# A fused state-space and feed-forward kernel: six gate/up tiles of the first 256 tokens ahead of the rest, with two token tiles transposed by DMA

## The chip, the cores and the metric

The kernel runs on one core of one Trainium2 chip. The metric is the device time of one execution in microseconds (us). A core has five engines that each run their own instructions in order: TensorE (PE, with its weight loads PEld), VectorE (DVE), ScalarE (ACT), GpSimd (POOL) and SyncE (SP). DMAs are issued from an engine's queue (SPq, ACTq, POOLq) and moved by 16 DMA engines.

## What is computed

```python
x = A_x                                   # [1, 2048, 512] bf16
xn = layernorm(x)                         # over the last axis, eps 1e-5
# A: diagonal complex state space, 512 states
dt = exp(log_dt); Lam_bar = exp(dt * Lam); B_bar = ((Lam_bar - 1) / Lam)[:, None] * Bmat
Bu = einsum("bld,pd->blp", xn, B_bar)
h[t] = Lam_bar * h[t-1] + Bu[:, t]        # 2048 steps
y = 2 * einsum("blp,dp->bld", h, Cmat).real + xn * Dskip
# B: feed-forward, hidden width 1376
z = (silu(xn @ w_gate) * (xn @ w_up)) @ w_down
out = x + y + z
```

All inputs and the output are bf16.

## The kernel before

**Tiles.** The 2048 tokens are 16 token tiles of 128 and 4 chunks of 512. The hidden width of 1376 is 10 feature tiles of 128 and a last one of 96. A feature tile of a chunk takes 8 matmuls with 512 columns: 4 for gate and 4 for up, one for each 128 of the 512 inputs (`gateup_tile`, L491; `gu_mm`, L429). ScalarE then empties the two banks of PSUM, gate through silu into `guT` and up as a copy into `u2` (`gu_out`, L440), and VectorE multiplies the two for a pair of feature tiles at once (L451). B-projection (`bproj_tile`, L352) is 8 such groups of 4 matmuls a chunk, each emptied by ScalarE (L359). PSUM has a pool of 8 banks (L69), and every matmul group takes its bank from it (`bank()`, L73).

**The head, tokens 0 to 511** (L599 to L684). PE starts with 9 dummy matmuls of 512 columns, while the first token tile is loaded. The norm of token tiles 0 to 3 runs on VectorE and ScalarE (`ln_stats`, L184; `rstd_act`, L188: Ln with a bias tile `eps_t`, then Exp; `norm_dve`, L201). Each of the four tiles is transposed on PE (`xT_pe`, L213: four transposes of 128x128, two to a bank), and the banks are copied to `xnT` by VectorE or ScalarE (L227, L229). Three feature tiles (H = 3) are begun at once, in six held banks (`held`, L603): `head_mm` (L627) gives one of gate and up a range of token tiles, in an order written out by hand (L635 to L671), so that PE has work as each token tile arrives. The transpose of the parameter rows (`prm_transpose`, L249) stands in the same bank as one of these. When token tile 3 is in, the held tiles are finished and emptied one by one (L679 to L683). Feature tiles 3 to 6 of chunk 0 follow (L741), then B-projection of chunk 0 (L745), then tiles 7 to 10 (L760).

**The parameters.** `params_a`, `params_a2` and `params_sin` (L252 to L312) make the decay and the angles; on ScalarE they are two Exp, one load of an activation table (L259) and two Sin, all ahead of the first silu. `params_b` (L314) is 17 small operations on VectorE that make the factors of C; they are used by `c_ops` (L331), which make `CF` ahead of the first `out_ssm` (L538).

**The planner.** Work of VectorE and ScalarE that isn't tied to a matmul group (the norm of the other chunks, the sine tables, the rotations and scans, the C factors) lies in `backlog` as pairs of a cost and an operation. After each group of matmuls `pump(us)` (L580) adds the group's PE time to `owed` and takes operations from the front of the backlog while `owed` is at least half the cost of the next one. `multiply` (L588) does the products that are due and takes 0.65 off `owed` for each. `need(tag)` (L594) empties the backlog up to a tag. So the emitted order of VectorE and ScalarE follows from the costs and from the order of the groups on PE.

**The queues.** SP issues nearly all loads (L123 to L148): x of tiles 0 and 2, gate and up of the weight groups, x of tiles 4 to 7, eight transposing loads of the B matrices into `BT` (L142), the last weights (`w_last`, L147). ScalarE issues x of tiles 1 and 3 and the first up group (L125 to L129). The weights lie in groups of feature tiles (`fgroups`, L88: 2, 1, 4 and 3 tiles). Token tiles 4 and on are transposed by DMA from SP (`xT_dma`, L232), as their norm is done; `load_late` (L150) and the transposes of C (L766) follow on SP.

## Time and profile before

| what | value |
|---|---|
| time, median of 3 | 179.23 us (179.14 to 179.45) |
| span of the profiled execution | 177.3 us |
| PE busy | 172.9 us, 97% of the span |
| DVE, ACT, POOL busy | 154.4, 94.7, 23.2 us |
| first transpose on PE | 4.76 us |
| first matmul with 256 columns | 7.68 us |
| load of the second activation table | 10.00 us, 1.28 long |
| first silu | 11.51 us |
| first matmul of feature tile 3 | 11.73 us |
| first matmul of feature tile 6 | 16.91 us |
| first matmul of B-projection | 18.64 us |
| DMA transposes of token tiles 4 to 7 issued | 20.06 to 25.2 us |
| DMA | 15.53 MB in 29131 packets |

The profile is of one execution, and its span goes from the first to the last instruction of the program; the time of an execution is 1.9 us longer. Times in the views are counted from the start of the span. "L631" is line 631 of the kernel before. A row of a group gives busy time, the mean length of one instruction in ns, and the idle time of the engine ahead of it with the one that ended it. Matmuls overlap, so the mean length of one isn't what it costs in a row of many.

### The profile page before, as it was taken

How to read it: one execution, taken by the hardware profiler on the slowest of the kernel's cores; microseconds unless marked ns; L12 is line 12 of the kernel's file. 1: busy time of each engine (PE TensorE's matmuls, PEld its weight loads, DVE VectorE, ACT ScalarE, POOL GpSimd, SP SyncE). 2: the span in 40 equal slices, each digit the busy share in tenths (PEclk: the TensorE clock that was granted, in tenths of full speed). 3: DMA queues.
4: the chain of work that ended last, by engine and by line, in shares of the span. 5: the costliest groups of instructions: out<-in, count | busy, mean ns of one | idle time of the engine just before them, and what ended most of it. 6: DMA issues, size and time to landing. Idle time of an engine off the chain costs nothing.

```text
span 177.3 us, 2449 instructions
## 1 busy us (share of the span) xinstructions
PE 172.9 (97%) x900; PEld 83.6 (47%) x916; DVE 154.4 (87%) x238; ACT 94.7 (53%) x173; POOL 23.2 (13%) x29
## 2 busy tenths in 40 slices
PE   8999999999999999999999999999999999999993
PEld 2884444444444444444444444444444444444743
DVE  6789997999999977899999999999999999990033
ACT  4589696977499369914966662013766600220000
POOL 6003000001200140000700000014280000150000
DMA  5999749973041024900440000005469500072012
GB/s 163 316 264 239 148 90 261 334 126 89 0 96 26 0 52 96 355 0 0 60 62 2 0 0 4 0 0 61 58 97 177 86 0 0 0 85 33 4 50 69
DMA packets 29131, 15.53 MB, mean 88 GB/s; under 512 B 18848, under 2 KB 29056, under 8 KB 29088
## 3 DMA queue, kind: packets, MB, share of 16 engines
q1 hardware_dynamic: 24416, 11.41, 28.8%
q0 software_dynamic: 3456, 3.28, 13.7%
q10 hardware_dynamic: 1248, 0.69, 1.3%
q8 instruction: 7, 0.11, 0.3%
q14 instruction: 4, 0.03, 0.1%
HBM read 8.03 MB, written 5.24 MB: 75 GB/s over the span
## 4 chain that ended last, share of the span: by engine, by line
PE 98%; issue 1%; DVE 0%
PE ps L432 36%; PE ps L528 19%; PE ps L545 16%; PE ps L357 16%; PE ps L631 3%; PE ps L608 2%; PE ps L483 2%; PE ps L535 2%; PE ps L472 1%; PE ps L220 1%; DVE res L548 0%; PE ps L250 0%
## 5 line engine op out<-in xcount | busy, mean ns | idle before, releaser
L432 PE MATMUL ps<-xnT,wg 128*128 128x512 bf16 x144 | 37.8, 379 | 0.4
L432 PE MATMUL ps<-xnT,wu 128*128 128x512 bf16 x145 | 37.3, 379 | 0.0
L528 PE MATMUL ps<-wd_sb,guT 128*128 128x512 bf16 (+2 forms) x177 | 36.7, 355 | 0.2
L399 DVE TENSOR_TENSOR_SCAN g<-r_t,car,u 128x512 bf16<-128x512 f32 x24 | 28.8, 1264 | 0.0
L545 PE MATMUL ps<-CF,wt 128*128 128x512 bf16 (+2 forms) x141 | 28.2, 355 | 0.2
L357 PE MATMUL ps<-xnT,BT 128*128 128x512 bf16 x126 | 28.2, 379 | 0.1
L446 ACT ACTIVATE guT<-ps 128x512 bf16<-128x512 f32 x40 | 24.6, 615 | 5.0 <-PE ps L432 5.0
L447 ACT CAST u<-ps 128x512 bf16<-128x512 f32 x40 | 24.1, 602 | 5.2 <-PE ps L432 5.1
L528 PEld LDWEIGHTS <-guT 128*128 128x128 bf16 x180 | 16.9, 98 | 18.0
L432 PEld LDWEIGHTS <-wu 128*128 128x128 bf16 x148 | 14.5, 98 | 17.5
L432 PEld LDWEIGHTS <-wg 128*128 128x128 bf16 x148 | 14.4, 98 | 17.2
L555 ACT CAST res<-ps 128x512 bf16<-128x512 f32 x12 | 6.7, 594 | 28.1 <-PE ps L545 28.1
L556 POOL DMA_DIRECT2D out_dram<-res x12 | 10.5, 1041 | 78.0 <-ACT res L555 78.0
L545 PEld LDWEIGHTS <-wt 128*128 128x128 bf16 x144 | 13.4, 98 | 14.4 <-issue 0.4
L357 PEld LDWEIGHTS <-BT 128*128 128x128 bf16 x128 | 12.5, 98 | 15.1
L359 ACT CAST u<-ps 128x512 bf16<-128x512 f32 x32 | 17.6, 588 | 3.7 <-PE ps L357 3.6
L451 DVE TENSOR_TENSOR guT<-guT,u 128x1024 bf16<-128x1024 bf16 x20 | 13.5, 680 | 0.0
L548 DVE TENSOR_TENSOR res<-ps,xn_end 128x512 bf16<-128x512 f32 (+2 forms) x6 | 3.0, 514 | 11.8 <-PE ps L545 11.8
L195 POOL TENSOR_TENSOR rstd<-ve,neg_half 128x4 f32<-128x4 f32 x3 | 5.3, 1761 | 53.9 <-DVE ve L194 53.9
L367 DVE TENSOR_TENSOR pm<-u,c 128x2048 bf16<-128x2048 bf16 x8 | 9.8, 1221 | 1.2 <-ACT c L284 1.1
L185 DVE BATCH_NORM_STATS2 stats<-xall 128x6 f32<-128x512 bf16 x14 | 9.5, 676 | 0.4 <-DMA xall<-in_A_x_dram 0.4
L367 DVE TENSOR_TENSOR pm<-g,c 128x2048 bf16<-128x2048 bf16 x8 | 9.7, 1215 | 0.1
(108 smaller groups left out, 166.6 us busy)
## 6 DMA issues: line engine op xcount, KB each, us to landing
out_dram<-in_A_x_dram SPq DMA_DIRECT2D x1, 1536.0 KB, 7.0
out_dram<-res POOLq DMA_DIRECT2D x12, 128.0 KB, 3.0
out_dram<-xall POOLq DMA_DIRECT2D x3, 512.0 KB, 7.6
wd_sb<-in_B_w_down_dram SPq DMA_DIRECT2D x1, 1280.0 KB, 10.9
xall<-in_A_x_dram SPq DMA_DIRECT2D x1, 1024.0 KB, 6.1
xall<-in_A_x_dram SPq DMA_DIRECT2D x2, 256.0 KB, 4.6
wg<-in_B_w_gate_dram SPq DMA_DIRECT2D x1, 512.0 KB, 5.6
wu<-in_B_w_up_dram SPq DMA_DIRECT2D x1, 512.0 KB, 6.1
```

What stands on the lines that cost most here:

```text
L185: nc.vector.bn_stats(out=stats[:, n, :], in_=xall[:, n, :])
L357: nc.tensor.matmul(ps[:], lhsT=BT[:, part, k, q * 128:(q + 1) * 128], rhs=xnT[:, k, c * CW:(c + 1) * CW], start=(k == 0), stop=(k == KD - 1))
L359: nc.scalar.copy(out=u_tiles[c][:, part, q, :], in_=ps[:])
L367: V.tensor_tensor(out=t[:], in0=flat(src()[:, i]), in1=flat(tab[:]), op=ALU.mult)
L399: V.tensor_tensor_scan(out=g()[:, part, q, :], data0=r_t[:, q:q + 1].to_broadcast([128, CW]), data1=u_tiles[c][:, part, q, :], initial=ini ...
L432: nc.tensor.matmul(ps[:fs, lo:hi], lhsT=wslice(groups, fi, k), rhs=xnT[:, k, c * CW + lo:c * CW + hi], start=(k == 0), stop=(k == KD - 1))
L446: nc.scalar.activation(out=guT[:fs, fi, :], in_=psg[:fs], func=ACT.Silu)
L447: nc.scalar.copy(out=u_pair[c][:fs, fi % 2, :], in_=psu[:fs])
L451: products.append(lambda: V.tensor_tensor(out=g, in0=g, in1=u, op=ALU.mult))
L528: nc.tensor.matmul(o[:], lhsT=gu_tiles[c][:, fi, i * 128:(i + 1) * 128], rhs=wd_sb[:, fi, lo:hi], start=(fi == 0), stop=False)
L545: nc.tensor.matmul(o[:], lhsT=w_tiles[c][:, part, q, i * 128:(i + 1) * 128], rhs=CF[:, part, q, lo:hi], start=False, stop=(c > 0 and part ...
L556: nc.gpsimd.dma_start(out=out_v[:, n, :], in_=res[:], accum_op=ALU.add)
```

## The change

It re-orders the head. Six feature tiles instead of three are begun in the six held banks, as three pairs (0, 2), (1, 3), (4, 5): a bank now holds one of gate and up for two feature tiles and 256 tokens, where it held one feature tile and 512 tokens. First all six are computed for tokens 0 to 255; then `head_out` empties a pair's two banks for that half, and the pairs are computed for tokens 256 to 511 in banks taken again from the pool (`second`). Products are done by half, with 512 elements instead of 1024.

Token tiles 2 and 3 are transposed by DMA from SP, not on PE. The norm of tiles 0 and 1 is done in two halves of 256 columns, and both copies of tile 0 are VectorE's, both of tile 1 ScalarE's. The bias of the Ln is the number 1e-5 instead of a tile.

Loads: the weight groups have 2 feature tiles each; ScalarE issues groups 1, 2 and 3, with group 2 between the two `rstd_act` of tiles 0 and 1 and group 3 after that of tile 3. SP issues, behind the two transposes, x of tiles 4 to 7 in one DMA, the eight transposing loads of B, and group 4. `w_last` is issued by GpSimd, out of the backlog. `params_b` moves to GpSimd, except for its reciprocal. The backlog begins with one table operation ahead of the norm's statistics, and eight feature tiles instead of seven stand ahead of B-projection.

```diff
-    fgroups = [(0, 2), (2, 3), (3, 7), (7, FT - 1)]
+    fgroups = [(0, 2), (2, 4), (4, 6), (6, 8), (8, FT - 1)]
...
-    load_w1(nc.sync, wg_g, wg_v, 1)
-    load_w1(nc.sync, wu_g, wu_v, 1)
+    load_w1(nc.scalar, wg_g, wg_v, 1)
+    load_w1(nc.scalar, wu_g, wu_v, 1)
...
+    def load_mid():
+        nc.sync.dma_start(out=xall[:, TPC:2 * TPC, :], in_=x_v[:, TPC:2 * TPC, :])
+        for part, src in enumerate((A_B_re, A_B_im)):
+            for k in range(KD):
+                nc.sync.dma_start_transpose(out=BT[:, part, k, :], in_=src[:, k * 128:(k + 1) * 128])
+        load_w1(nc.sync, wg_g, wg_v, 4)
+        load_w1(nc.sync, wu_g, wu_v, 4)
+
+    def load_w_last():
+        nc.gpsimd.dma_start(out=w_last[:, :, 0:LB + LA], in_=wg_v[:, :, FL:F])
+        nc.gpsimd.dma_start(out=w_last[:, :, LB + LA:128], in_=wu_v[:, :, FL + LB:F])
...
-        nc.scalar.activation(out=ve[:, n:n + 1], in_=mv[:, n, 1:2], func=ACT.Ln, bias=eps_t[:, 0:1])
+        nc.scalar.activation(out=ve[:, n:n + 1], in_=mv[:, n, 1:2], func=ACT.Ln, bias=EPS)
...
     def params_b():
+        G = nc.gpsimd
...
-        tt(t_a[:], lre, lre, ALU.mult)
+        gt(t_a[:], lre, lre, ALU.mult)
...
         V.reciprocal(out=den[:], in_=den[:])
...
+    def head_mm(sets, fis, which, lo, hi, ks=range(KD)):
+
+        base = lo * 128 // HALF * HALF
         for fi in fis:
+            p, j = place[fi]
             for k in ks:
+                nc.tensor.matmul(sets[p][which][:, j, lo * 128 - base:hi * 128 - base],
+                                 lhsT=wslice((wg_g, wu_g)[which], fi, k),
                                  rhs=xnT[:, k, lo * 128:hi * 128], start=(k == 0), stop=(k == KD - 1))
...
+    def head_out(sets, p, half):
+
+        if half == 0:
+            head_u[p] = up_p.tile([128, 2, CW], BF16, name="u2")
+        cols = slice(half * HALF, (half + 1) * HALF)
+        a, b = pairs[p]
+        g, u = gu_tile(0)[:, a:b + 1:b - a, cols], head_u[p][:, :, cols]
+        nc.scalar.activation(out=g, in_=sets[p][0][:], func=ACT.Silu)
+        nc.scalar.copy(out=u, in_=sets[p][1][:])
+        products.append(lambda: V.tensor_tensor(out=g, in0=g, in1=u, op=ALU.mult))
...
     ln_stats(0)
     rstd_act(0)
+    load_w1(nc.scalar, wg_g, wg_v, 2)
     nc.vector.bn_stats(out=stats[:, 1, :], in_=xall[:, 1, :])
-    norm_dve(0)
+    norm_dve(0, 0, DH)
+    norm_dve(0, DH, D)
     nc.vector.bn_aggr(out=mv[:, 1, :], in_=stats[:, 1, :])
     rstd_act(1)
-    xT_pe(0, on_dve=(0,))
-    dummy(4, 128)
-    norm_dve(1)
+    load_w1(nc.scalar, wu_g, wu_v, 2)
+    xT_pe(0, 0, True)
+    dummy(1, 128)
+    xT_pe(0, 1, True)
+    dummy(3, 128)
+    norm_dve(1, 0, DH)
+    norm_dve(1, DH, D)
     ln_stats(2)
+    head_mm(held, (0, 1), 0, 0, 1, kh[0])
+    head_mm(held, (0, 1), 0, 0, 1, kh[1])
+    xT_pe(1, 0, False)
+    head_mm(held, (0, 1), 1, 0, 1, kh[0])
+    xT_pe(1, 1, False)
+    head_mm(held, (0, 1), 1, 0, 1, kh[1])
     rstd_act(2)
     nc.vector.bn_stats(out=stats[:, 3, :], in_=xall[:, 3, :])
     norm_dve(2)
+    xT_dma(2)
     nc.vector.bn_aggr(out=mv[:, 3, :], in_=stats[:, 3, :])
     rstd_act(3)
+    norm_dve(3)
+    xT_dma(3)
+    load_w1(nc.scalar, wg_g, wg_v, 3)
+    load_w1(nc.scalar, wu_g, wu_v, 3)
+    load_mid()
+    head_mm(held, (0, 1), 0, 1, 2, kh[0])
+    head_mm(held, (0, 1), 1, 1, 2, kh[0])
+    head_mm(held, (0, 1), 0, 1, 2, kh[1])
+    head_mm(held, (0, 1), 1, 1, 2, kh[1])
+    head_mm(held, (2, 3), 0, 0, 2)
+    pp = prm_transpose()
+    head_mm(held, (2, 3), 1, 0, 2)
     params_a(pp)
     params_a2()
     params_sin()
+    head_mm(held, (4, 5), 0, 0, 2)
+    head_mm(held, (4, 5), 1, 0, 2)
     tables = table_ops()
     stats1, norm1 = ln_rest(1, False)
-    queue("ln1", stats1)
-    queue("tables", tables[:2])
+    queue("tables", tables[:1])
+    queue("ln1", stats1 + [(0.0, load_w_last)])
+    queue("tables", tables[1:2])
     queue("ln1", norm1)
     queue("tables", tables[2:])
+    second = []
+
+    def more():
+        second.append((bank((128, 2, HALF)), bank((128, 2, HALF))))
+
+    more()
+    head_out(held, 0, 0)
+    head_mm(second, pairs[0], 0, 2, 3)
+    head_mm(second, pairs[0], 1, 2, 3)
+    pump(GU / 2)
+    more()
+    head_out(held, 1, 0)
+    head_mm(second, pairs[1], 0, 2, 3)
+    head_mm(second, pairs[1], 1, 2, 3)
+    pump(GU / 2)
+    multiply(1)
+    head_out(held, 2, 0)
+    for p in range(2):
+        head_mm(second, pairs[p], 0, 3, 4)
+        head_mm(second, pairs[p], 1, 3, 4)
+        head_out(second, p, 1)
+        pump(GU / 2)
+        multiply(1)
+    more()
+    head_mm(second, pairs[2], 0, 2, 4)
+    head_mm(second, pairs[2], 1, 2, 4)
+    head_out(second, 2, 1)
+    pump(GU)
+    multiply(1)
...
-    G0 = 7
-    for fi in range(H, G0):
+    G0 = 8
+    for fi in range(2 * NP, G0):
```

More of the change, by code (lines that the diff above doesn't have):

```diff
@@ L211, with xT_pe @@
     HK = KD // 2
-    def xT_pe(n, on_dve=(), prm_too=False):
+    def xT_pe(n, h, on_dve):
         c, i = divmod(n, TPC)
-        for h in range(2):
-            tp = bank((128, HK * 128 + 128), BF16)
-            for k in range(HK):
-                lo = (h * HK + k) * 128
-                nc.tensor.transpose(out=tp[:, k * 128:(k + 1) * 128], in_=xn_tile(c)[:, i, lo:lo + 128],
-                                    identity=ident[:])
-            if prm_too and h == 1:
-                prm_transpose(tp[:, HK * 128:])
-            dst = xnT[:, h * HK:(h + 1) * HK, n * 128:(n + 1) * 128]
-            src = tp[:, 0:HK * 128].rearrange("p (k t) -> p k t", k=HK)
-            if h in on_dve:
-                nc.vector.tensor_copy(out=dst, in_=src)
-            else:
-                nc.scalar.copy(out=dst, in_=src)
-        return tp[:, HK * 128:]
+        tp = bank((128, HK * 128), BF16)
+        for k in range(HK):
+            lo = (h * HK + k) * 128
+            nc.tensor.transpose(out=tp[:, k * 128:(k + 1) * 128], in_=xn_tile(c)[:, i, lo:lo + 128], identity=ident[:])
+        dst = xnT[:, h * HK:(h + 1) * HK, n * 128:(n + 1) * 128]
+        src = tp[:].rearrange("p (k t) -> p k t", k=HK)
+        if on_dve:
+            nc.vector.tensor_copy(out=dst, in_=src)
+        else:
+            nc.scalar.copy(out=dst, in_=src)
     def xT_dma(n):
@@ L247, with prm_transpose @@
     V = nc.vector
-    def prm_transpose(pp):
-        nc.tensor.transpose(out=pp, in_=prm_rows[:], identity=ident[:])
+    def prm_transpose():
+        pp = bank((128, 128), BF16)
+        nc.tensor.transpose(out=pp[:], in_=prm_rows[:], identity=ident[:])
+        return pp
     def params_a(pp):
@@ L601 @@
     BP = 4 * 0.2163
-    H = 3
-    held = [(bank(), bank()) for _ in range(H)]
-    warm = held[0][0]
+    NP = 3
+    HALF = CW // 2
+    held = [(bank((128, 2, HALF)), bank((128, 2, HALF))) for _ in range(NP)]
+    warm = held[0][0][:].rearrange("p a b -> p (a b)")
     def dummy(n, cols):
@@ L684 @@
-    pump(2.0)
+    second = []
[19 more added lines that the diff above has]
+        multiply(1)
```

80 lines of the change are left out of this document (25 added, 55 removed).

## The prediction

> **What bounds the kernel now.** I read the page's busy times first, then the chain that ended last, then the waits, then the timeline of the first 20 us with that of TensorE's neighbours.
>
> ```profile
> PE 172.9 (97%) x900; PEld 83.6 (47%) x916; DVE 154.4 (87%) x238; ACT 94.7 (53%) x173; POOL 23.2 (13%) x29
> ...
> PE 98%; issue 1%; DVE 0%
> ```
>
> TensorE is the chain: nothing that another engine does is on it. All waits of PE until 40 us come to one, the start (0.8 us), and the chain in order of time has PE from 0.78 to 174.54. So the change can win only what it takes out of PE's own stream, or out of the small gaps at the start, and it loses whatever new wait it puts there. From the chain in order of time and the groups by shape:
>
> ```profile
> 4.78 0.59 PE ps L220 x4
> ...
> 8.28 0.22 PE ps L220 x4
> ...
> 9.66 0.22 PE ps L220 x4
> 9.88 2.01 PE ps L631 x36
> ...
> 25.71 5.18 PE ps L432 x24
> ```
>
> Columns: start, length, what. The rows give the price of one instruction in the stream: 2.01/36 = 0.056 us for 128 columns, 0.22/4 = 0.055 for a transpose, 5.18/24 = 0.216 for 512 columns. The 256-wide ones start four in 0.437 us (7.68 to 8.11 in the timeline): 0.109 each. The "mean" of the group of transposes (0.241 us) isn't the price: they overlap.
>
> ```profile
> 7.68 0.60 PE L631 MATMUL ps<-xnT,wg 128*128 128x256 bf16 x4
> ...
> 9.35 0.21 ACT L254 ACTIVATE dt_t<-prm 128x4 f32<-128x4 f32 x1 [0.81 <-DVE prm L253]
> ...
> 10.00 1.28 ACT L259 ACT_TABLE_LOAD   x1
> ...
> 11.51 0.58 ACT L446 ACTIVATE guT<-ps 128x512 bf16<-128x512 f32 x1
> ...
> 11.73 1.03 PE L432 MATMUL ps<-xnT,wg 128*128 128x512 bf16 x3
> ...
> 20.06 5.16 SPq L234 DMA_TRANSPOSE xnT<-xall  x4
> ```
>
> Here the reader is to see ScalarE: its first silu comes at 11.51, straight behind the table load, and no bank of `held` comes free before that. The last line prices a DMA transpose: 1.29 us of SP each; from issue to landing it took 2.4 us (all four alike, on a quiet queue).
>
> **The change, part by part.** I sum up to one mark: the first matmul of tile 6, now at 16.91 us. The profiled span is 177.3 us; the three timed executions took 179.14 to 179.45 (median 179.23), so some 1.9 us lie around the span, and I add them unchanged.
>
> *The start to the first 256-wide matmul (now 7.68).* The bias of the Ln becomes a number: the Ln with `eps_t` took 0.298, the Exp with no tile of bias 0.203, so 0.09 sooner. The half norm: 0.41 us for 512 elements and 0.17 for the 4 elements of the small tensor_scalars give 0.29 for 256, so 0.12 sooner. Together the first transposes could start 0.21 before 4.76, but the nine dummies (0.427 apart from 0.78) hold PE to 4.57: 0.18 sooner. Most of it goes again: both copies of tile 0 now stand behind each other on VectorE (0.21 from start to start), and tile 1's halves wait for them. Copies end 5.33 and 5.64; gate 5.39 and 5.70; tile 1's first half is transposed at 5.92, copied by ScalarE in 0.37 to 6.61; the 16 matmuls of tokens 128-255 run 6.66 to 7.55. Won: 0.12 (between 0 and 0.2).
>
> *Transposes.* Eight leave PE: 8 x 0.056 = 0.45 won. Here a rule stands against the row. The Trainium skill ("TensorE: Matmul & The Clock Gate", Part 4: PE-mode transpose) puts one transpose at about 275 ns in a kernel. Were that the price in the stream, eight would be 2.2 us and the time 177.3; the row of four in 0.22 us excludes it here, so it gets no chance.
>
> *Shapes.* Tiles 0-5 go from 80 x 0.0558 + 8 x 0.109 + 24 x 0.2155 = 10.51 to 96 x 0.0558 + 48 x 0.109 = 10.59: 0.09 lost.
>
> *The new wait.* From 7.55: tiles 2, 3 (16 x 0.109), the parameters' transpose, tiles 4, 5 (16 x 0.109) reach 11.10; there token tile 2 is needed. Pair 0 on tile 2 (16 x 0.0558) goes into the two banks left of eight and ends at 12.00. Pair 1 needs the banks of `held[0]`, which ScalarE must empty first. Queued on ScalarE ahead of that: rstd of tile 3 (ends 8.5), now two DMA issues of 0.46 (its own three issues were 0.43 and 0.49 apart), so dt_t at 9.45 for 9.35 although its input is ready at 9.1; then the same 2.16 us to the silu (9.35 to 11.51): 11.63. It takes 0.58, PE sees it 0.06 later: 12.27; the second bank at 12.74; all of PE's stream is queued behind this wait. PE waits 0.27 + 0.02 = 0.29. Even with no DMA issue on ScalarE the silu is at 11.3 or so and the wait about zero; that is the good end. On: 12.74 + 0.45 = 13.19 (tile 3 needed), + 2 x 0.89 = 14.98, + 1.75 = 16.73.
>
> Sum: -0.12 - 0.45 + 0.09 + 0.29 = **-0.19 us** at the mark: 179.04, say 179.05.
>
> *The loads on ScalarE's queue.* Needed: gate of group 1 by 7.55, up 8.42, group 2 by 9.35 and 10.22. In the trace's packet records 1.1 MB had landed by 5.5 us at about 300 GB/s; four more 256 KB loads at that rate land near 6.4, 7.3, 8.2, 9.1: hidden by 1 us. The other end: at 213 GB/s (the 128 KB loads of 256-byte pieces, 6.2 to 7.4) they land at 6.8, 8.0, 9.2, 10.5, 0.3 late. I take the first; the new pieces have 512 bytes, as the first loads.
>
> *Token tiles 2 and 3 by DMA.* Norm 2 ends at 7.94, issue 8.0, landing 2.4 later on a quiet queue: 10.4, needed 11.10; another 0.27 is free because PE waits for the bank anyway, so 11.3 costs nothing. Tile 3: SP is free at 9.3, landing 11.7, needed 13.19. Four copies leave VectorE (0.29 each), unseen by PE.
>
> *SP behind that.* x of tiles 4-7 is issued at 10.6 for 3.25 and lands near 13.9 instead of 8.8; VectorE stands at its first statistics from 11.8 until then, and behind them the half products and the norms of tiles 4-7, which nobody needs before 21. Eight BT transposes at 1.3 follow to 21.5: the real half lands near 17.8 (needed by B-projection at 16.73 + 3.45 = 20.18), the imaginary one at 23.2 (its last before was 3.0 from issue to landing; needed 23.6), group 4 by 26 (needed 27.1), the transposes of tiles 4-7 by 29.3 (needed 31.3). GpSimd's two issues of `w_last` (0.5 to 0.7 each, as its other issues) stand behind its power for the norm, near 21; needed 30.6. All hidden, the imaginary half by least: 0.4 us.
>
> *VectorE and the planner.* params_b's 17 operations (31.99 to 34.02: 2.0 us) go to GpSimd, whose first three can run long before VectorE's reciprocal (with the rotations queued behind it) asks for them. GpSimd shows no such product; its nearest row, the power on 128x4, took 1.76: 17 of these are 30 us from about 21, still before the first use at 66; at VectorE's 0.16 it is nothing. Six half products for three whole ones cost 0.2. Following the planner's debts by hand, the second pair of sines is issued behind tile 9, so the first rotation moves from 29.7 to 33.0; params_b's leaving and the five evictions that no longer stand ahead of the cm operations give it back. The last CF starts near 73.9 (74.10 now), PE asks for it at 74.1 + 7 x 0.2155 = 75.6. No charge; without that cover each 1 us of VectorE beyond 1 us late costs PE the same.
>
> **Rivals.** Within 0.2% (0.36 us) is about what a measurement of this kernel can tell from no change.
>
> 1. *The bank wait doesn't occur* (ScalarE's issues short, or the silu sooner): -0.48, 178.75. For it: only 0.29 us of wait. Against it: 2.16 us of chain behind dt_t that nothing shortens. 0.10.
>
> 2. *Slower: token tile 2 or 3 lands late.* Before, transposes never shared the engines with loads of another queue. The nearest rows are the instruction fetches: one of 16 KB began at 12.11, and the transposes' packets in flight stood still from 12.55 to 14.01; again 0.9 us at 17.46 and 2.5 at 34.8. The place is the first matmul on tile 2, the point is a landing after 11.3. A stop of 1.46 puts it at 11.9: +0.55 against my sum, 179.6; one of 2.5, 180.7; 180.0 for both tiles hit. Against it: plain packets of 27 ns are not a fetch of 1.1 us. The Trainium skill ("DMA: Bandwidth & Descriptors", Queues, rings and completion order) says an engine alternates between queues packet by packet. As a mechanism here: 512 packets of 18 ns behind 512 of 27 ns on 16 engines add 0.9 us, landing 11.3, which still costs nothing: 179.05 to 179.1; that speaks for my forecast. 0.24.
>
> 3. *ScalarE is held by its DMA issues.* SP's issues took 1.17, 2.15 and 2.37 us where much was queued, for 0.46. At 1.17 each, wg3 and wu3 put dt_t at 10.9, the bank at 13.7: +1.4, 180.45. Where the two are issued the queue holds half of what it holds at 5 us, against it. With it go late weights or a late BT. 0.16.
>
> **How the numbers follow.** Forecast 0.50: 179.05, own range 178.85 to 179.35. Faster by over 0.2%: rival 1 and 0.04 of the forecast, 0.14. Same: 0.46 of the forecast, 0.04 of rival 2, 0.03 of rival 3: 0.53. Slower: 0.20 + 0.13 = 0.33. The range leaves out a few in 100 below rival 1 and the dear half of rivals 2 and 3: 178.75 to 180.3.
>
> **What would show it.** PE's first 256-wide matmul near 7.55; a wait of PE for a `ps` that ScalarE empties near 12.0 to 12.3; the first silu at 11.6; tile 2 landed by 11.1 and tile 3 by 13.1; tile 6 at 16.7; from there the same chain to the end. I am wrong if PE waits for xnT near 11.1, for a weight before, for BT near 20 or 23.6, for CF near 75, or if ScalarE's issues are longer than 0.5 us.

## The result and the profile after

The changed kernel takes 180.69 us (median of 4 runs, 180.49 to 180.94) where the kernel before takes 179.29 (median of 4): a ratio of 1.0081, 95% interval 1.0068 to 1.0094. It is 1.4 us slower. The forecast was 179.05, with a range up to 180.3; both were wrong. The profiled execution has a span of 178.7 us (177.3 before).

The page of the changed kernel, busy times and the chain that ended last:

```profile
PE 172.8 (97%) x925; PEld 85.2 (48%) x940; DVE 152.8 (86%) x224; ACT 96.0 (54%) x172; POOL 35.7 (20%) x48
...
PE 78%; DVE 9%; DMA 5%; ACT 4%; issue 2%
```

PE has as much to do as before. But the chain, which was PE's alone (98%), now runs for a fifth of the span through other engines and DMAs. In order of time (start, length, what):

```profile
7.83 4.11 DMA xnT<-xall
11.99 5.50 PE ps L635 x80
...
32.02 0.96 ACT s L278
32.97 0.95 ACT c L278
33.95 2.36 DVE pm L368 x2
...
53.87 0.71 ACT xall L205
55.03 2.45 DMA xnT<-xall
57.62 3.83 PE ps L358 x17
```

There are two places where something else ends last: PE waits at 11.99 for the DMA transpose of token tile 2, and at 57.62 for the last transpose of chunk 2, which hangs on a line of VectorE and ScalarE that begins with the sine tables at 32 us. Setting the starts of PE's instructions side by side with those of before, PE is 0.41 us behind at the first matmul of tile 6 (17.32 for 16.91), 0.51 behind B-projection of chunk 0, 0.99 behind 57.62, and the 0.99 stays to the end. The rest, 0.37 us, lies behind the last instruction of VectorE: from there to the end of the span (the tail, below) it is 2.86 us, before 2.49.

The head, from the timelines of PE and of ScalarE in the changed kernel:

```profile
7.53 1.04 PE L635 MATMUL ps<-xnT,wg 128*128 128x256 bf16 x8
...
11.99 0.62 PE L635 MATMUL ps<-xnT,wg 128*128 128x128 bf16 x8 [0.75 <-DMA xnT<-xall]
```

```profile
8.17 0.41 ACTq L112 DMA_DIRECT2D wg<-in_B_w_gate_dram  x1
8.62 0.68 ACTq L112 DMA_DIRECT2D wu<-in_B_w_up_dram  x1
...
11.50 0.58 ACT L646 ACTIVATE guT<-ps 128x512 bf16<-128x512 f32 x1
```

The first 256-wide matmul is at 7.53 (forecast 7.55) and the first silu at 11.50 (forecast 11.63), so ScalarE is on time. PE stands for token tile 2 and not for a bank: 0.92 us beyond the normal step. And the DMAs issued from 7.5 to 10.4 us (last column: us from issue to landing):

```profile
wg<-in_B_w_gate_dram ACTq DMA_DIRECT2D x1, 256.0 KB, 3.5
wu<-in_B_w_up_dram ACTq DMA_DIRECT2D x1, 256.0 KB, 3.9
xnT<-xall SPq DMA_TRANSPOSE x2, 4.0
```

The two transposes took 4.1 and 3.9 us, not 2.4. Their data were held up only a little: in the packet records the data of tile 2 moved between 9.1 and 10.4 us, 1.3 us long, where the same transpose with no load beside it (in the run "Every transfer of the head mended" below) needs 0.8. But its semaphore writes were sent at 10.7 to 11.0, and the semaphore rose at 11.69 to 11.94, 1.5 us behind the last data, where it is 0.45 us in that other run, and just behind the semaphore of wg3, the load on ScalarE's queue (11.46 to 11.67). Tile 3's rose at 13.13, behind that of wu3 (12.55). The Trainium skill ("DMA: Bandwidth & Descriptors", Queues, rings and completion order) says that a semaphore write lands only after every earlier write of that DMA engine, across its queues; the records agree.

Chunk 2's transposes, next. VectorE and ScalarE come to the norms of chunk 2 about 2.8 us later than before, and the last of the four norms ends at 54.59. The transposes ahead of it were slow in their turn, as these lines show: the DMA transposes issued by line 226 of the changed kernel (ns, shortest, median and longest issue; then the time to landing), and a queue of the DMAs from 49.5 to 56.3 us (packets, MB, share of time):

```profile
L226 SPq DMA_TRANSPOSE xnT<-xall x4: 1201/1218/2000, 49.6 to 55.0; - x4
DMA to landing us min/median/max: 2.4/2.9/4.3
```

```profile
q8 instruction: 1, 0.02, 1.4%
```

The one packet of q8 is a fetch of 16 KB of instructions, from 52.36 to 53.87 us. Packets of the transposes that were in flight beside it stood for 1.5 to 1.6 us, the second transpose took 4.3 us from issue to landing, and SP needed 2.00 us to issue the third, not 1.2. So the fourth went out at 55.03, 0.44 behind its norm, and not at once. In the run with three mends (below) the same norm ended at 54.58 with no fetch near it: the fourth was issued at 54.60, and PE didn't wait. So of PE's 0.49 us here some 0.41 come with the fetch; but it could cost this much only because the later order had used up the time that these transposes had to spare. It is the kind of stop that rival 2 took as its row, at another place.

**Theory** that the experiments start from, in which the fetch isn't a term: three costs, apart from each other. The head waits for a transpose whose completion stands behind loads of another queue; a later order of VectorE's and ScalarE's work makes chunk 2's transposes late; and the end is longer by the order of SP's last waits. **Rivals**: DMA transposes in the head are slow by themselves; VectorE is late because x of tiles 4 to 7 lands late or GpSimd is slow; the last stores are slow.

### The profile page after: what moved, and what is told of

It reads as the page before. It is cut to its first block, busy times and chain, and to the rows that moved or that the text cites. A ratio compares the mean times of both kernels' runs of the same rounds, so it can differ in the third digit from the quotient of the medians.

```text
span 178.7 us, 2511 instructions
## 1 busy us (share of the span) xinstructions
PE 172.8 (97%) x925; PEld 85.2 (48%) x940; DVE 152.8 (86%) x224; ACT 96.0 (54%) x172; POOL 35.7 (20%) x48
## 3 DMA queue, kind: packets, MB, share of 16 engines
q0 software_dynamic: 3536, 3.41, 14.6%
## 4 chain that ended last, share of the span: by engine, by line
PE 78%; DVE 9%; DMA 5%; ACT 4%; issue 2%
PE ps L433 23%; PE ps L529 19%; PE ps L546 15%; PE ps L358 12%; DMA xnT<-xall 4%; PE ps L635 4%; DVE pm L368 3%; PE ps L536 2%; DVE g L400 2%; DVE stats L182 2%; DMA xall<-in_A_x_dram 1%; ACT u L448 1%; PE ps L473 1%; ACT guT L447 1%; PE ps L484 1%
## 5 line engine op out<-in xcount | busy, mean ns | idle before, releaser
L433 PE MATMUL ps<-xnT,wg 128*128 128x512 bf16 x134 | 34.6, 379 | 0.2
L433 PE MATMUL ps<-xnT,wu 128*128 128x512 bf16 x133 | 34.3, 379 | 0.1
L447 ACT ACTIVATE guT<-ps 128x512 bf16<-128x512 f32 x34 | 20.4, 601 | 5.8 <-PE ps L433 5.7
L448 ACT CAST u<-ps 128x512 bf16<-128x512 f32 x34 | 20.1, 590 | 6.4 <-PE ps L433 6.4
L360 ACT CAST u<-ps 128x512 bf16<-128x512 f32 x32 | 18.2, 589 | 7.3 <-PE ps L358 7.3
L433 PEld LDWEIGHTS <-wu 128*128 128x128 bf16 x136 | 13.3, 98 | 16.0
L433 PEld LDWEIGHTS <-wg 128*128 128x128 bf16 x136 | 13.3, 98 | 15.8
L452 DVE TENSOR_TENSOR guT<-guT,u 128x1024 bf16<-128x1024 bf16 x17 | 11.4, 675 | 0.0
```

The costliest lines, as they stand in the source:

```text
L360: nc.scalar.copy(out=u_tiles[c][:, part, q, :], in_=ps[:])
L433: nc.tensor.matmul(ps[:fs, lo:hi], lhsT=wslice(groups, fi, k), rhs=xnT[:, k, c * CW + lo:c * CW + hi], start=(k == 0), stop=(k == KD - 1))
L447: nc.scalar.activation(out=guT[:fs, fi, :], in_=psg[:fs], func=ACT.Silu)
L448: nc.scalar.copy(out=u_pair[c][:fs, fi % 2, :], in_=psu[:fs])
L452: products.append(lambda: V.tensor_tensor(out=g, in0=g, in1=u, op=ALU.mult))
```

## The experiments

All times are medians, ratios are to the kernel before on the same chip; the changed kernel stands at 1.0081.

### Weight group 3 issued later

```diff
-    load_w1(nc.scalar, wg_g, wg_v, 3)
-    load_w1(nc.scalar, wu_g, wu_v, 3)
...
     params_a2()
+    load_w1(nc.scalar, wg_g, wg_v, 3)
+    load_w1(nc.scalar, wu_g, wu_v, 3)
     params_sin()
```

> The changed kernel, but ScalarE issues its two loads of weight group 3 only behind its work on the parameters (behind its last table load, near 11 us) instead of at 8.0 and 8.5 us. Theory: the DMA transposes of token tiles 2 and 3 were late because their completion had to pass behind those two loads on the same DMA engines. Then tile 2, issued at 7.8, lands after about 2.4 us, near 10.3 (11.94 with the loads ahead), tile 3 near 12 (13.13), PE doesn't wait for xnT at 11, and the first matmul of feature tile 6 comes near 16.4 to 16.7 (17.32); the time falls by 0.4 to 0.7 us against the changed kernel, less what a later BT or group 3 costs. Rival: two DMA transposes issued one behind the other beside any load land in 4 us; then tile 2 stays near 11.9 and tile 6 near 17.3, time unchanged.

Measured: 182.17 us, 1.0162 (1.0146 to 1.0177). Tile 2 landed 2.6 us after its issue and PE didn't wait for it, as the theory says. But the loads went out at 9.59 and 10.16, beside tile 3's transpose, which now took 4.0 us (landed 13.42, wg3's 13.21): tile 6 at 16.99, 0.33 won. Then x of tiles 4 to 7 landed at 16.97 (14.56), and PE waited 0.9 us in B-projection of chunk 1 and 1.5 in that of chunk 2. The wait follows the loads from one transpose to the next; on the total it is a miss, 1.5 us longer than the changed kernel where 0.4 to 0.7 less was expected, and the time is lost behind the head.

### A load beside transposes, at a quiet place

```diff
-        nc.sync.dma_start(out=xall[:, 2 * TPC:NT, :], in_=x_v[:, 2 * TPC:NT, :])
...
             def one(n=n):
+                if n == TPC:
+                    nc.scalar.dma_start(out=xall[:, 2 * TPC:NT, :], in_=x_v[:, 2 * TPC:NT, :])
```

> The kernel before, with its load of x of token tiles 8 to 15 (1 MB) issued by ScalarE at the time of the first transpose of token tiles 4 to 7 and not by SP behind the fourth: a load of another queue beside DMA transposes, at a place where the transposes took 2.4 us each from issue to landing. Theory (a transpose lands late because its completion stands behind the packets of another queue's load): the first transposes land 4 us or more after their issue, each near the time when the load's packets end, and those issued behind the load's end land in 2.4 us again. Rival (the 4 us belong to the start of the kernel, or to two transposes in a row): all four stay at 2.4 to 2.7 us.

Measured: 182.11 us (one run). ScalarE issued the load at 16.7, earlier than meant, so it met the last transposes of B too. The DMAs issued from 16 to 24 us, and those issued from 24 to 28, in that kernel:

```profile
xall<-in_A_x_dram ACTq DMA_DIRECT2D x1, 1024.0 KB, 8.3
w_last<-in_B_w_gate_dram SPq DMA_DIRECT2D x1, 96.0 KB, 6.7
BT<-in_A_B_im_dram SPq DMA_TRANSPOSE x3, 7.8
w_last<-in_B_w_up_dram SPq DMA_DIRECT2D x1, 32.0 KB, 6.2
xnT<-xall SPq DMA_TRANSPOSE x1, 5.9
```

```profile
xnT<-xall SPq DMA_TRANSPOSE x4, 2.5
```

Two transposes of B landed 8.1 and 7.8 us after their issue (24.49 and 25.48), around the landing of the load (25.06); plain loads of SP suffer alike, even one of 32 KB; of the four transposes of the second view, the one issued at 20.39 took 5.9 us, and the three issued from 24.3 on took 2.4 to 2.5 (the rows give medians). PE waited 2.3 us for BT. That decides the first point, by the landings and not by the time of a single run: transposes land late beside another queue's load, wherever in the kernel. The first of them was done at 24.49, a little ahead of the load's own landing.

The profile of before held a row near to it. The transposes of C were issued from 29.3 us behind the loads of w_down, though on the same queue, so that it shows what a crowd costs and not what another queue does; of the DMAs issued from 29 to 43 us before the change:

```profile
CT<-in_A_C_re_dram SPq DMA_TRANSPOSE x4, 6.2
CT<-in_A_C_im_dram SPq DMA_TRANSPOSE x4, 2.7
```

The first three landed at 37.99, 38.48 and 38.99, right behind w_down (37.55), 8.7, 6.8 and 5.6 us after their issue.

### Transposes on PE

```diff
     norm_dve(2)
-    xT_dma(2)
+    hold(2)
...
+    xT_pe(2, 0, True)
     pp = prm_transpose()
+    xT_pe(2, 1, True)
```

(`hold` is a DMA of 128 bytes from SP that needs the norm of its tile; tile 3 likewise, between the matmuls of tiles 4, 5.)

> The changed kernel with token tiles 2 and 3 transposed on PE as before the change (16 transposes, half of them of this part; copies on VectorE); two tiny DMAs that wait for the norms of tiles 2 and 3 stand in SP's queue in place of the two DMA transposes, so that what follows them doesn't start early and the count of DMAs is the same. Theory: PE's wait of 0.92 us for xnT goes and 8 transposes at 0.056 us come back: tile 6 near 16.85 (17.32), SP is 1.6 us sooner with BT, whose small wait goes: 180.1 us. Rival: the head is late for another reason (banks, ScalarE's silu), then tile 6 stays at 17.2 or later and the time at 180.7.

Measured: 180.79 us, 1.0079 (1.0062 to 1.0095). From the first up matmul to tile 6 it is 10.91 us, for 11.26 in the changed kernel: 0.35 won, where the sum 0.92 - 0.45 - 0.1 says 0.37. But the first up weights landed at 6.31 (6.01), so that all began 0.30 later, and chunk 2's wait was 0.66 for 0.49 (there the fourth transpose went out 0.03 behind its norm, at 55.07, so that wait is the order's and not the fetch's). The time didn't move: a miss on the total. In the profile the later start and the longer wait of chunk 2 took what the head had won.

### Every transfer of the head mended

```diff
     def load_mid():
+        load_w1(nc.sync, wg_g, wg_v, 3)
+        load_w1(nc.sync, wu_g, wu_v, 3)
...
             bproj_tile(0, part, q)
+            if part == 0 and q == 2:
+                load_w1(nc.scalar, wg_g, wg_v, 4)
+                load_w1(nc.scalar, wu_g, wu_v, 4)
```

(with the two mends of the next sections)

> The changed kernel with each found cost taken away: weight group 3 issued by SP behind the transpose of token tile 3 (so that nothing is in flight beside the two transposes but what went before them), group 4 issued by ScalarE inside B-projection (so that SP isn't later for it), wu_last by GpSimd (56 DMAs), and the planner's half products at half price. Theory: tile 2 lands near 10.4 and tile 3 near 12.1, PE has at most 0.15 us of wait for a bank, tile 6 near 16.5 (17.32 in the changed kernel, 16.91 before); no wait of 0.5 us in B-projection of chunk 2, tail 2.45 us; about 179.1 us, as before the change or a little under. Rival: every transfer that is put ahead in the head makes another late, and the waits come back at BT or at the transposes of token tiles 4 to 7; then 179.8 us or more.

Measured: 182.42 us, 1.0165 (1.0149 to 1.0181). With nothing in flight beside them, both transposes took 2.5 us (10.43 and 11.81), PE didn't wait, and tile 6 came at 16.45: the best head of all, 0.46 sooner than before the change. Then the load that ScalarE issued at 22.70 (landed 26.16) held the last transpose of B, issued at 22.38, to 26.36. PE's waits in that kernel:

```profile
PE ps L358 <- DMA BT<-in_A_B_im_dram: 2.1, 1, 2.1
```

The rival was right: the head's gain is real, but its price is a crowd of transfers elsewhere.

### The end: which semaphore comes last

The tail is the time from the end of VectorE's last instruction to the end of the span. The DMAs of SP and ScalarE take their semaphores from eight in turn. At the end SP waits for the eight in a fixed order, 0.063 us each. Before, the last store had the last of them; with 57 DMAs it has the first in the order, and seven waits follow its landing.

```diff
-        nc.sync.dma_start(out=wu_last[:], in_=wu_v[:, :, FL:FL + LB])
+        nc.gpsimd.dma_start(out=wu_last[:], in_=wu_v[:, :, FL:FL + LB])
```

> The changed kernel, but the small late load of wu_last is issued by GpSimd and not by SP: SP and ScalarE together issue 56 DMAs as before the change, not 57. Theory: at the end SP waits one behind the other, about 0.063 us each, for the eight semaphores that these DMAs take in turn; with 57 the last store has the first in the order, so seven waits follow its landing, with 56 it has the last. Then the stretch from the last VectorE instruction to the end of the span falls from 2.86 to about 2.45 us and the time by 0.4 us. Rival: the tail is longer because the last stores land later, which has nothing to do with the count; then it stays at 2.86 us.

Measured: 180.20 us, 1.0059 (1.0040 to 1.0078), with the tail at 2.43 us. The last store landed at 177.21 and SP's last wait ended at 177.26; in the changed kernel 177.34 and 177.82. SP's waits at the end for the stores, in the changed kernel and in this one (us, times, longest):

```profile
SPq L866 <- DMA out_dram<-res: 1.1, 1, 1.1
```

```profile
SPq L866 <- DMA out_dram<-res: 0.5, 2, 0.4
```

In the first SP stands once, for the last store, with all other waits behind it; in the second it waits as the stores come. The other way round, in the kernel before:

```diff
-        nc.sync.dma_start(out=xall[:, 2 * TPC:NT, :], in_=x_v[:, 2 * TPC:NT, :])
+        for n in (2 * TPC, 3 * TPC):
+            nc.sync.dma_start(out=xall[:, n:n + TPC, :], in_=x_v[:, n:n + TPC, :])
```

> The kernel before, with its load of x of token tiles 8 to 15 cut into two DMAs, so that SP and ScalarE issue 57 and not 56. Theory of the order of the semaphores at the end: the stretch from the last VectorE instruction to the end of the span grows from 2.49 to about 2.9 us, the time by 0.4 us (179.3 to 179.7). Rival: a load that nobody waits for costs nothing: no change.

Measured: 180.13 us, 1.0046 (1.0034 to 1.0058), 0.9 us and not 0.4. PE's stream is as before to 0.1 us; the tail is 3.44 us. SP's last wait ended 0.52 us behind the last landing (0.04 before), which is the theory's 0.4 to 0.5; the rest is a second stop of 0.47 us in SP's last steps (177.02 to 177.49), of which the profiles of before, of the changed kernel and of the run with one DMA less have one each; its cause isn't shown. So the number of DMAs set 0.4 to 0.5 us in either direction.

### The planner: half price, a table first, three mends, four mends

The rotation below is the first of VectorE's operations on the sines and cosines (`pm<-u,c`); it marks how late VectorE's line is.

`multiply` charges 0.65 for each half product, which takes 0.4. The first run gives back half of it, the second puts a table operation into the 2.9 us for which VectorE stands for x of tiles 4 to 7:

```diff
+    owed[0] += 6 * 0.325
     G0 = 8
```

> The changed kernel, but the planner gets back half of what it is charged for the six half products (6 x 0.325 us on the planner's account). Theory: that charge is why the norms of token tiles 8 to 11 are emitted later, their last transpose lands at 57.5 and PE waits 0.5 us for it; then the second rotation comes near 46.8 as before (48.6), the last transpose lands near 55, the wait goes and the time falls by 0.3 to 0.5 us. Rival: VectorE itself is late, from the late landing of x of tiles 4 to 7 and from GpSimd's slow parameter work; then the order moves but the last transpose still lands after 57 and the time stays.

Measured: 180.81 us, 1.0083 (1.0068 to 1.0098). In the profile the last transpose landed at 56.58 (57.48) and PE was 0.60 sooner there; 0.30 of it went again near 74, where PE waited for the transposes of tiles 12 to 15. Of the 0.90 by which the transpose was sooner, 0.45 comes from a sooner norm; the rest goes with the fetch, which came at 57.66 here, behind the transposes. In the timed runs nothing is left.

```diff
-    queue("tables", tables[:1])
+    queue("tables", tables[:2])
```

> The changed kernel with one more operation of the sine tables (1.9 us of VectorE) ahead of the statistics of token tiles 4 to 7 in the planner's list, so that VectorE has work in the 2.9 us in which it stands for x of these tiles. Theory: VectorE's standing is what makes the tables, then the first rotation (33.95 us, before 29.71), then the norms of token tiles 8 to 11 late, and PE's wait in B-projection of chunk 2 with them; the first rotation comes near 32, the last transpose of chunk 2 lands near 55.6 (57.48) and the wait is gone: 0.4 to 0.5 us sooner, near 180.2. Rival: the order in which the planner emits, not VectorE's standing, sets it: the first rotation stays at 33.5 or later and the time at 180.7.

Measured: 180.55 us, 1.0076 (1.0061 to 1.0091). The first rotation stayed at 33.87: the rival. VectorE then stood for ScalarE's halves (0.88, 0.55) and for GpSimd's power (1.16) instead.

> The changed kernel with three mends that leave the head's transfers as they are: the table operation first, the half products at half price, wu_last issued by GpSimd (56 DMAs). Theory: what is left against before is the head's wait for token tile 2 alone: no wait in B-projection of chunk 2, tail 2.45 us instead of 2.86; 179.7 us. Rival: the work that VectorE and ScalarE have to do behind the head has no room, so that the wait comes back later (for CF near 75 us): 180.2 us or more.

(both edits and the end's.) Measured: 180.28 us, 1.0059 (1.0045 to 1.0073). Chunk 2's wait was gone, the tail short, but PE waited 0.5 us near 74: the rival's kind of wait, though for tiles 12 to 15 and not for CF. That the wait of chunk 2 went is not the edits' doing alone, for the last norm ended where it did in the changed kernel (54.58); what was missing is the fetch, as the DMA queues from 49.5 to 56.3 us show, with no row of q8:

```profile
xnT<-xall SPq DMA_TRANSPOSE x4, 2.4
```

> The same three mends and token tiles 2 and 3 transposed on PE (with the two tiny DMAs that hold SP's queue as the transposes did). Theory: a saving in the head is kept once chunk 2's transposes are in time; PE's wait of 0.92 us goes against 0.45 us of transposes and some 0.1 us for banks: tile 6 at 16.9 to 17.2, about 179.3 to 179.5 us, which is the kernel before. Rival: the saving is swallowed by a later wait as in the run with the transposes on PE alone: 179.7 us as with three mends.

(the same with the transposes on PE.) Measured: 180.16 us, 1.0054 (1.0039 to 1.0068): the rival again, and the theory's 179.3 to 179.5 a miss. In the profile the first up weights landed at 6.71, and near 74 PE waited 0.67. Of PE's weight loads in that kernel:

```profile
PEld L635 <- DMA wu<-in_B_w_up_dram: 0.7, 1, 0.7
```

### x of tiles 4 to 7 sooner

```diff
     load_w1(nc.scalar, wu_g, wu_v, 2)
+    nc.scalar.dma_start(out=xall[:, TPC:2 * TPC, :], in_=x_v[:, TPC:2 * TPC, :])
...
+    nc.gpsimd.tensor_scalar(out=hold[:], in0=rstd[:, 3:4], scalar1=1.0, scalar2=None, op0=ALU.mult)
+    load_w1(nc.gpsimd, wg_g, wg_v, 3)
+    load_w1(nc.gpsimd, wu_g, wu_v, 3)
```

> The changed kernel with x of token tiles 4 to 7 issued by ScalarE behind the loads of weight group 2 (near 5.7 us instead of 10.5 by SP), and weight group 3 issued by GpSimd behind a tiny operation on rstd of token tile 3, so that about as much is in flight beside the transposes of tiles 2 and 3 as in the changed kernel; SP and ScalarE issue 55 DMAs. Theory: VectorE's whole line of work behind the head is full, so its first statistics (14.59 us, before 11.19) set the first rotation (33.95, before 29.71) and the norms of token tiles 8 to 11 and 12 to 15: the statistics begin near 12, the first rotation near 31.5, the last transpose of chunk 2 lands near 55, PE doesn't wait there nor near 74; the tail is 0.35 us shorter; PE's wait for token tile 2 stays or grows by some tenths: 179.8 to 180.2 us. Rival: the half products and the planner's order make the lateness, and the first rotation stays near 33.9 although the statistics are sooner; then 180.4 us or more.

Measured: 182.61 us (182.20 to 184.16), 1.0219 (1.0184 to 1.0254). The transpose of tile 3 landed 6.6 us after its issue (15.96; wu3, now on GpSimd's queue, 16.05), and PE waited 3.0 us in the head. VectorE's first statistics began at 11.53, but the others stood until 18.1 behind half products that wait for ScalarE and PE. The question was hidden by this wait; what it adds is that a transpose lands late beside a load on GpSimd's queue too.

### VectorE's work and the order, apart and together

```diff
-        products.append(lambda: V.tensor_tensor(out=g, in0=g, in1=u, op=ALU.mult))
+        products.append(lambda: None)
```

> The changed kernel without the six half products of feature tiles 0 to 5 of chunk 0 (silu(gate) isn't multiplied by up there; that work of VectorE, 6 x 0.39 us, is left out); the planner charges for them as before, so the order of all other work is the same. Theory: VectorE's line is full; the first rotation comes 1.5 to 2.3 us sooner, near 32, the last transpose of chunk 2 lands near 55.5, PE's wait of 0.5 us goes and no wait near 74 takes its place: near 180.2 us. Rival: the emitted order and ScalarE's sines hold it: rotation at 33.5 or later, wait and time (180.7) unchanged.

Measured: 180.66 us, 1.0067 (1.0054 to 1.0080), not told from the changed kernel. This version leaves the half products out. The rotation came 13.1 us behind the first matmul of B-projection (13.2 in the changed kernel). VectorE's tables had nothing to wait for but ScalarE:

```profile
28.44 0.70 DVE L273 TENSOR_SCALAR pm<-pm 128x1024 f32<-128x1024 f32 x1 [1.61 <-ACT s L278]
```

ScalarE's sines stand in its own line behind evictions that PE's groups set; so taking away VectorE's work alone moves the rotation by 0.1 us, and half price alone by 0.3. The next run gives the products to GpSimd (`nc.gpsimd.tensor_tensor`):

> The changed kernel with the six half products on GpSimd instead of VectorE. Theory: as without them, if GpSimd's multiply of 128x512 takes about 1 us and doesn't hold up its power for the norm of tiles 4 to 7 (19.85 us): near 180.2 us. Rival: GpSimd is so slow at them, or slows VectorE so much, that the norm of tiles 4 to 7 is late and PE waits for their transposes near 31.5: 181 us or more.

Measured: 180.75 us, 1.0079 (1.0067 to 1.0091), rotation at 13.1 again; the theory missed. With the end's mend and the transposes on PE besides:

> The half products on GpSimd, wu_last by GpSimd (56 DMAs) and token tiles 2 and 3 transposed on PE with two tiny DMAs in the place of theirs in SP's queue. Theory: with all three costs taken off (head 0.4, chunk 2 0.5, tail 0.4) the six-tile head is worth what the kernel before is: 179.2 to 179.5 us. Rival: the start of the head (the first up weights land between 5.9 and 6.7 and PE asks for them at 6.05, before at 6.27) or a late wait keeps 0.4 us or more: 179.7 us or more.

Measured: 180.55 us, 1.0070 (1.0052 to 1.0087). Tile 6 came at 17.28, the rotation at 13.6, and PE waited 0.60 in chunk 2. A miss; the charge of the planner was as before in all three. Then charge and work were taken off together:

```diff
+        def product():
+            nc.gpsimd.tensor_tensor(out=g, in0=g, in1=u, op=ALU.mult)
+            owed[0] += 0.65
+        products.append(product)
```

> The changed kernel with the six half products on GpSimd and not charged by the planner, and wu_last by GpSimd (56 DMAs). Theory: the order (the planner's charge) and VectorE's work are the two bounds of the first rotation; with both taken off it comes 11.1 to 11.6 us behind the first matmul of B-projection (13.2 in the changed kernel, 11.07 before the change), the last transpose of chunk 2 lands at least 1.2 us sooner, and PE waits neither there nor for token tiles 12 to 15 near 74: about 179.7 us with the shorter tail. Rival: a third bound (GpSimd's power for the norm, ScalarE's evictions) holds the rotation at 12.8 or more, or the wait comes back near 74: 180.2 us or more.

Measured: 180.86 us, 1.0100 (1.0080 to 1.0120), rotation at 13.7: the rival, and a new reason. VectorE's four norms of tiles 4 to 7 in this kernel:

```profile
20.43 4.18 DVE L200 TENSOR_SCALAR xall<-xall,mv,rstd 128x512 bf16<-128x512 bf16 x4
```

They came 1.2 to 1.4 us apart (0.32 in the changed kernel), while GpSimd issued its DMAs and did two products of 1.16 us. A sine, now ahead of evictions in ScalarE's line, stood 4.1 us for VectorE's tables behind them, and the evictions stood behind it.

> The same with token tiles 2 and 3 transposed on PE and two tiny DMAs in their place in SP's queue. Theory: with the waits behind it gone, what the head saves is kept (0.92 us of waiting against 0.45 us of transposes and up to 0.5 us for late first up weights): 179.3 to 179.6 us. Rival: PE waits later for what it has saved: 179.7 us or more.

Measured: 181.60 us, 1.0128 (1.0110 to 1.0146), with a sine that stood 5.1 us and PE behind it:

```profile
PE ps L433 <- ACT u L360: 0.9, 1, 0.9
```

The last run leaves GpSimd out of it: `product` only gives back the charge.

> The changed kernel with the six half products left out (that work is missing) and not charged by the planner; GpSimd has no more to do than in the changed kernel. Theory: VectorE's norms of tiles 4 to 7 take 0.4 to 0.6 us each again, and with order and work both taken off the first rotation comes 11.1 to 12.0 us behind the first matmul of B-projection (13.2 in the changed kernel, 13.1 with the work alone taken off, 12.9 with half price alone), the last transpose of chunk 2 lands at least 1.2 us sooner than in the changed kernel and PE doesn't wait for it: near 180.2 us. Rival: a third bound holds the rotation at 12.8 or more.

Measured: 180.26 us, 1.0052 (1.0038 to 1.0066). VectorE in this kernel:

```profile
20.96 1.76 DVE L200 TENSOR_SCALAR xall<-xall,mv,rstd 128x512 bf16<-128x512 bf16 x4
...
32.66 1.22 DVE L368 TENSOR_TENSOR pm<-u,c 128x2048 bf16<-128x2048 bf16 x1 [1.12 <-ACT c L278]
```

The rotation came 11.25 us behind the first matmul of B-projection (before the change 11.07), the last transpose of chunk 2 landed at 55.27, and PE waited neither there nor near 74. That fits the theory: the emitted order and VectorE's work are two bounds of nearly the same height, and each alone hides what the other gives. One side of it rests on one run with half the charge given back: no version gives back the whole charge and keeps the products on VectorE. In that run VectorE has no idle time of note from 14.6 to 32.5 us, and ScalarE stands for it:

```profile
32.54 1.06 ACT L278 ACTIVATE c<-pm 128x1024 bf16<-128x1024 f32 x1 [1.32 <-DVE pm L274]
```

On the time the last run is told from the changed kernel (1.0068 to 1.0094), but not from the run without half products (1.0054 to 1.0080). And its fetch of instructions came at 56.88, behind the transposes.

### The sooner start alone

```diff
-        ... func=ACT.Ln, bias=eps_t[:, 0:1])
+        ... func=ACT.Ln, bias=EPS)
...
-    norm_dve(0)
+    norm_dve(0, 0, D // 2)
+    norm_dve(0, D // 2, D)
```

(in the kernel before; tile 1 likewise)

> The kernel before with two small parts of the change alone: the bias of Ln is a number, and the norms of token tiles 0 and 1 are done in two halves of 256 columns. Theory: the first matmuls come 0.1 to 0.2 us sooner, no wait takes it back since nothing else waits for those engines, and the time falls by 0.1 to 0.2 us, at the edge of what can be measured. Rival: PE in the head waits for a later link (silu at 11.5, weights), and the time is unchanged.

Measured: 179.19 us, 0.9992 (0.9982 to 1.0001): no difference that these runs can tell. The first matmul came at 5.40 (5.54), but in the profile the first up weights landed at 6.36 and PE waited for them: tile 3 began at 11.81 (11.73). There the gain ends at the next link. None of the versions beats the kernel before.

## Why the prediction was wrong, point by point

*Head to 7.55, transposes, shapes.* Right: 7.53; without its wait, PE's way to tile 6 was as summed, 5.33 us from token tile 2 on. What it left out is the first up group: PE now asks for it at 6.05 instead of 6.27, and it landed between 5.85 and 6.71 in the profiles with this head. The list of needed loads began at group 1.

*The bank wait of 0.29.* Didn't occur: the silu came at 11.50, and PE came later still. *Rival 3*, ScalarE held by its issues, didn't happen: they took 0.41 and 0.68 us. The second is beyond the 0.5 that the prediction names as a sign of being wrong, but the silu was on time all the same. One of its three rows, the 2.37 us, is the issue of a DMA transpose, which takes 1.2 to 1.3 us in any case, and not 0.46.

***Token tiles 2 and 3 by DMA*: the first step that failed.** "Landing 2.4 later on a quiet queue: 10.4" was 11.94, needed 11.10. Rival 2 had the place, the point (11.3) and nearly the price (+0.55 against the sum; tile 6 came 0.59 later than forecast), with a chance of 0.24, but by another mechanism: not a stop of the packets of 1.5 us, but a completion behind wg3's. That the price came near is luck. The step took the four quiet transposes as its row and passed over the transposes of C in the same profile (8.7 us behind w_down, on their own queue). It also weighed the packets' turns and not the completion's: it put 0.9 us on 512 packets between, the data were held by 0.5, and the semaphore came 1.5 us behind the data, where 0.45 is the measure with nothing beside it. The runs that put the load beside transposes at another place, or took it away, show that the load does it; that it is the completion is read from the packet records.

*SP behind that, all hidden.* Nearly: BT's last landed at 24.91 (forecast 23.2), and PE's wait was 0.1 us; x of tiles 4 to 7 at 14.56 (13.9).

***VectorE and the planner: no charge*: the second step that failed.** First rotation 33.95 (forecast 33.0), before 29.71. What was to give it back, params_b's leaving and the five evictions, gave back 1.2 of the 4.2 us up to the norms of tiles 12 to 15. And the step followed the lateness to CF, which had cover, but not to the transposes of chunk 2: these had a slack of 2.3 us (landed 54.30, needed 56.62) and came 3.2 us later, while PE came 0.5 later. Of the 3.2, the lateness of the norms is 2.8; that is the whole slack and PE's 0.5 besides, to within 0.1. The other 0.4 come with the fetch of instructions at 52.36, which stopped the transposes. GpSimd's slow params_b was no part of it; it ended at 40.7 us. Size: 0.49 us in the profile, some 0.41 of it with the fetch. The profiles of four other versions have such a fetch between 52 and 53 us too, others have it near 50 or behind 54; what places it isn't shown, nor how often it falls there in the timed runs. The run with both bounds taken off has 1.0052 for 1.0081.

***1.9 us around the span and the tail unchanged*: the third.** One DMA more of SP and ScalarE cost 0.4 to 0.5 us at the end (1.0059 without it, against 1.0081). The sum had no term for it. The 1.9 us themselves held (1.8 now); what failed is "the same chain to the end", in the tail inside the span.

Together 0.41 at tile 6, 0.1 at BT, 0.4 to 0.5 in chunk 2 and 0.4 to 0.5 at the end make the 1.4. The terms are read from one profile each. Not settled: how much of VectorE's lateness comes from x of tiles 4 to 7 landing 5.8 us later; the run for it was covered by the head's wait. Nor was a six-tile head tried whose B matrices are loaded ahead of it.

## What to carry to other kernels

Price a DMA by what else is in flight until it has landed, on all queues, and take the row from the most crowded place of the profile, not from the quietest: its completion can come behind the loads beside it. When a part of the head is re-ordered, follow the planned work of the other engines to every place where PE takes something from them, and ask for two bounds of like height: an experiment that takes off one of them shows little. Write down how much time the transfers on the way have to spare, and don't let a change use it all: a stop of 1.5 us that was hidden before then costs PE. Count the DMAs: here one more or less moved the end by 0.4 to 0.5 us.

## What the runs showed of the hardware

- A DMA transpose's semaphore rose late beside a load of another queue, near that load's own landing: from issue to landing it took 4 us beside loads of 256 KB, up to 8 us beside one of 1 MB, 6.6 us beside one on GpSimd's queue, 2.4 to 2.6 us with nothing beside it.
- VectorE's norm of 128x512 (0.40 us) took 1.47, 1.30 and 1.24 us in a row while GpSimd issued DMAs and did products of 128x512 (1.16 us each). The second and the third ended 0.1 to 0.2 us behind the end of a product; the first ran beside DMA issues, beside which alone norms took 0.4 to 0.64 us in other runs, so that what held it stays open. The Trainium skill ("SBUF — State Buffer", SBUF: two separate sides) says that the two share a pair of ports that one of them holds for a whole instruction; the second and the third norm agree with it. GpSimd's 128x4 operations took 0.2 to 1.3 us, VectorE's 0.16.
- At the end of the program SP waited for eight DMA semaphores in a fixed order, 0.063 us each.
- A fetch of 16 KB of instructions stopped the packets of DMA transposes in flight for 1.5 us (changed kernel, from 52.36 us); before the change, packets in flight beside such fetches stood 1.46 us (12.55 to 14.01) and 2.5 us (at 34.8).
- The landing of the first up group varied by a microsecond (5.7 to 6.7) between executions that issue it at the same time.
